# An mLSTM cell and a gated MLP in one kernel: who issues the loads of xT, and where five kinds of small steps stand in the order

## The chip, the cores and the metric

The kernel runs on one core of a Trainium2 chip. A core has five engines that run beside each other: TensorE (PE in the profile; its weight loads are PEld), VectorE (DVE), ScalarE (ACT), GpSimd (POOL) and SyncE (SP), which here only issues DMAs. Each engine works through its own instructions in the order in which they were written; an engine that must wait for another stands still until the semaphore arrives, and with it all that is queued behind. The metric is the device time of one launch in microseconds, lower is better; the times shown are medians of several runs.

## The reference

An mLSTM cell over 4 batches, 8 heads, 768 time steps and heads of 40 numbers, and behind it an MLP on the result, seen as 3072 tokens of 320 features:

```python
for t in range(S):
    m_new = np.maximum(f_gate[:, :, t] + m, i_gate[:, :, t])
    f_stab, i_stab = np.exp(f_gate[:, :, t] + m - m_new), np.exp(i_gate[:, :, t] - m_new)
    C = f_stab * C + i_stab * outer(v_t, k_t)      # 40 x 40 for each batch and head
    n = f_stab * n + i_stab * k_t
    h = C @ q_t
    y_t = sigmoid(o_gate_t) * h / np.maximum(np.abs(n @ q_t), 1.0)

x = y as (3072, 320)
h = x @ w_in                                       # 320 -> 2048
out = (h - np.tanh(h)) @ w_out                     # 2048 -> 320
```

## The kernel before, in words

**Units and groups.** The cell is cut into 24 units of 128 time steps of one batch (unit n is chunk n // 4 of batch n % 4). Within a unit the recurrence is a masked product of scores, P, with scaled values, vs, plus the product of the queries with the state that the batch's last unit left. Two units make a group of 256 tokens for the MLP; there are 12 groups. A group's input, transposed to features by tokens, is xT. The MLP works on the 2048 hidden features in 8 pairs of 128 + 128; an *item* is two pairs of one group: products up (ph_up <- xT, w_in), the polynomial for h - tanh(h) on ScalarE and VectorE (z, q, gt), products down (pS <- w_out or weight sums, gt or sums of gt), which run one item later.

**Seven products for eight.** From group 4 on, the 2 x 2 blocks of the up product and of the down product are computed with seven products in place of eight. That needs sums of weights (sum_w_in writes part or sums_in; sums_of_weights writes wT), sums of the inputs (sum_x, into freed xT buffers) and sums of gt (sums_of_g, s), all on VectorE.

**Two stretches.** The first 12 units and the first four groups are put in order by a small planner (class Plan) that simulates the engines. The second stretch, from item START = 17 on (about 203 us in the trace), is written out by a loop: for each item x it has a list of TensorE steps with costs (dense) and a list of other steps with places (work[x]), and merge() walks through both; a step placed at START + 0.8 comes when 0.8 of the first item's cost is through. Clock.later(key, us, step) holds a step back until that many microseconds of cost have been issued, or until Clock.need(key) asks for it.

**Slots.** In the second stretch the 12 units 12 to 23 pass through slots two items long (about 18.7 us). cell_slot(s, o) starts unit s (its loads, the scaling of its values in prepare) and finishes unit o, the one before: its four gate steps (gate_turned: den, o, ys, ys) and turn_by_store. A slot has 21 places (the last, which starts no unit, 20). For unit s the scores are computed in the slot's first item (crossed_scores: products ps, then two masks on VectorE that write P), and in the second item block_turned computes the state products (pT) and the products of P and vs.

**Through DRAM.** The unit's result stands in a layout with heads apart. turn_back transposes blocks of it on VectorE (zt), stores them with four DMAs (h_rows) and loads them again with four (z_in), all issued by SP. The gate steps of the next slot read z_in. turn_by_store then transposes y by blocks (yt), stores it with four DMAs (y_rows) and loads it as xT with three (96, 64 and 32 KB), these too issued by SP. SP's order in a slot is: loads of the next unit, y_rows of the unit before, xT of the unit before, h_rows of the slot's unit, z_in.

**GpSimd** has two memsets per slot in this stretch: zeros behind k, when the next unit's loads are issued, and zeros behind vs (the padding of the values), in block_turned.

**The order of an engine** is kept by a wrapper (Pinned, T) that chains every instruction to the one before on its engine; so nearly all instructions carry the wrapper's lines in the profile, L106 for VectorE, ScalarE, GpSimd and SP, L129 and L133 for TensorE. The names of tiles tell them apart.

**Banks.** An item's up products fill two PSUM tiles (X and Y in up_in_seven). Two adds (both), two squares (z) and two cubes (gt <- ph_up, z) read them; when the cubes and adds are through, the next item's first up product may write there:

```python
            square_b = square(z[0][:, 1], b, 0)
            add_d = V.tensor_tensor(out=both[:, 0], in0=d, in1=cs, op=OP.add)
            after(square(z[0][:, 0], a, 1), add_d)
            after(V.tensor_tensor(out=both[:, 1], in0=e, in1=cs, op=OP.add), square_b)
```

The masks of a new unit are issued right behind these lines, and steps given to Clock.later come behind the masks.

Of the kernel before, what the change touches and what calls it, by code (L numbers as in the profile page):

```python
# [60 lines left out]
L = 128  # L61
# [18 lines left out]
def kernel(  # L80
# [188 lines left out]
    B, NT, D, H, _ = qT.shape  # L269
    D1 = D + 1  # L270
# [6 lines left out]
    NK = 2  # L277
# [352 lines left out]
    def begin(n):  # L630
        if n in ld:
            arrive(n)

        un[n]["P"] = att.tile([L, 2, HH, L], FP, name="P", tag="P", bufs=4)
# [5 lines left out]
    def prepare(n, whole=True, by_heads=False):  # L640

        t = un[n]
        if "vs" in t:
            return
        t["vs"] = scaled(n, 0, "vs", 4, by_heads)
        if whole:
            t["column"]()
            open_gate(n)
# [147 lines left out]
    def turn_by_store(n):  # L796

        y, g, tt = un[n]["y"], *divmod(n, GT)  # L800
        yt = att.tile([L, NB, BLOCK], FP, name="yt", tag="yt", bufs=1)
        flat = yt.rearrange("p b j -> p (b j)")
        V.transpose(flat[:, 0:NK * 128], y[:, 0:NK * 128])
        V.transpose(flat[:, NK * 128:], y[:, FROM[NK]:DM])
        rows = dram.tile([DM, L], FP, name="y_rows", tag=f"y_rows{n % 4}")
        for a in range(L // BLOCK):
            part = slice(a * BLOCK, (a + 1) * BLOCK)
            SP.dma_start(out=rows[:, part].rearrange("(b i) j -> i b j", i=BLOCK), in_=yt[part])
        for i in range(2):
            half, to = slice(i * HALF, (i + 1) * HALF), xT[slot_of(g)][i * HALF:(i + 1) * HALF, :, tt * L:(tt + 1) * L]  # L810
            if i == 0:
                SP.dma_start(out=to, in_=bass.AP(rows.tensor, rows.offset, [[L, HALF], [128 * L, NK + 1], [1, L]]))
            else:
                SP.dma_start(out=to[:, 0:NK], in_=rows[0:NK * 128].rearrange("(c p) t -> p c t", p=128)[half])
                SP.dma_start(out=to[:, NK], in_=rows[FROM[NK]:])

    def in_halves(b):

# [10 lines left out]
    def block_turned(n):  # L829

        t = un[n]
        G.memset(t["wide"][:, H * D1:], 0.0)
        old = state[t["b"]][(t["c"] + 1) % 2].rearrange("p h d -> p (h d)")

        t["turned"] = [ps_a.tile([128, 2 * 2, L], FP, name="pT", tag=f"a{i}") for i in range(2)]
        for g in range(2):
            for c in range(2):
                for i in range(2):  # L840
                    rows, j = slice(i * HALF, i * HALF + D), 2 * g + c
                    T.matmul(t["turned"][i][c * HALF:(c + 1) * HALF, i * 2 + g, :], old[rows, j * D1:j * D1 + HALF], t["qz"][rows, j, :],
                             start=(g == 0), stop=False, skip_group_check=True)
        for i in range(2):
            P = over_diagonal(t["P"], i)
            for kind, half in ((0, 0), (1, 0), (0, 1), (1, 1)):
                for c in range(2):
                    g, r = i ^ kind, half ^ kind
                    rows, at = slice(r * HALF, (r + 1) * HALF), (i * HH + 2 * g + c) * D1
                    to = t["turned"][r][c * HALF:(c + 1) * HALF, i * 2 + g, half * HALF:]  # L850
                    T.matmul(to if half else to.rearrange("d (two t) -> d two t", two=2), t["wide"][rows, at:at + HALF],
                             P[rows, 1 + kind, c] if half else P[rows, 0:2 + kind:1 + kind, c], start=False, stop=True, skip_group_check=True)
        update_halves(n)
# [68 lines left out]
    def cell_slot(s, o):  # L922


        steps, pause = [], [(0.0, lambda: None)]
        if s is not None:
            if s + 1 < NU and s + 1 not in ld:
                load_unit(s + 1, ("kz", "qz", "v", "k", "o"), crossed=True)
            begin(s)
        if o is None:  # L930
            return [(0.0, lambda: prepare(s))]
        steps += 5 * pause
        if s is not None:
            steps.append((0.0, lambda: prepare(s)))
        steps += 6 * pause
        gates = []
        steps.append((0.0, lambda: [gates.extend(gate_turned(o)), gates[0]()]))
        steps += [(0.0, lambda i=i: gates[i]()) for i in range(1, 4)]
        steps.append((0.0, lambda: turn_by_store(o)))
        return steps + 4 * pause  # L940


    gT, po = {}, {}
# [18 lines left out]
    def sums_of_weights(p):  # L962
        if p % 2 == 0:
            both = conv.tile([128, 2, 4, HM], FP, name="wT", tag="w64", bufs=4)
            wT[p], wT[p + 1] = both[:, 0], both[:, 1]
        t = wT[p]
        even, odd = (w_out[:, 2 * p + i, :].rearrange("p (two n) -> p two n", two=2) for i in range(2))
        sub = OP.subtract
        return [(1.0, lambda o=o, a=a, b=b: V.tensor_tensor(out=o, in0=a, in1=b, op=sub)) for o, a, b in (
            (t[:, 0], even[:, 1], even[:, 0]), (t[:, 1], odd[:, 1], t[:, 0]),  # L970
            (t[:, 2], odd[:, 1], even[:, 1]), (t[:, 3], odd[:, 0], t[:, 1]))]
# [179 lines left out]
    def sum_w_in(p):  # L1151

        a11, a21, a12, a22 = (w_in[:, p, i * 128:(i + 1) * 128] for i in range(4))
        t = sums_in_of(p)
        both = w_in[:, p, 0:4 * 128].rearrange("p (j f) -> p j f", j=4)
        return [lambda: V.tensor_tensor(out=t[:, 0:4:2], in0=both[:, 1:4:2], in1=both[:, 0:2], op=OP.subtract),
                lambda: V.tensor_tensor(out=t[:, 1], in0=a22, in1=t[:, 0], op=OP.subtract),
                lambda: V.tensor_tensor(out=t[:, 3], in0=a12, in1=t[:, 1], op=OP.subtract)]
# [16 lines left out]
    def up_in_seven(x, some):  # L1175
# [43 lines left out]
        def shrunk():  # L1219
            both = conv.tile([128, 2, n, L], FP, name="both", tag="w_r", bufs=2)  # L1220
            z, q = ([mlp.tile([128, 2, n, L], FP, name=name, tag=name) for i in range(2)] for name in ("z", "q"))
            gt = gT[some] = [mlp.tile([128, 2, n, L], FP, name="gt", tag="gt", bufs=4) for i in range(2)]
            columns = [2 * x, 2 * x + 1, 2 * len(items) + x - START]

            def square(to, src, i):
                return A.activation(out=to, in_=src, func=AF.Square, accum_out=sums[:, columns[i]:columns[i] + 1])

            def again(i):
                A.activation(out=q[i], in_=z[i], func=AF.Square, bias=tiny)

            def cube(to, src, by):
                V.scalar_tensor_tensor(out=to, in0=src, scalar=TINY_POLY[0], in1=by, op0=OP.mult, op1=OP.mult)

            def last(i):
                V.scalar_tensor_tensor(out=gt[i], in0=q[i], scalar=TINY_POLY[2], in1=gt[i], op0=OP.add, op1=OP.mult)

            def after(later, sooner):
                tc.add_manual_dep(later.ins, sooner.ins.name, SYNC, reason="one engine at a bank")
# [5 lines that stand above are left out]
            again(0)  # L1244
            square(z[1], both, 2)
            again(1)
            early, late = (some, "early"), (some, "late")
            Clock.later(early, 1.0, lambda: cube(gt[0][:, 1], b, z[0][:, 1]))
            Clock.later(early, 1.1, lambda: cube(gt[0][:, 0], a, z[0][:, 0]))
            Clock.later(early, 1.9, lambda: last(0))  # L1250
            Clock.later(late, 2.6, lambda: cube(gt[1], both, z[1]))
            Clock.later(late, 3.3, lambda: last(1))
            Clock.later(some, 3.4, lambda: sums_of_g(some))
# [439 lines left out]
    def spread_over(steps, x0, x1):  # L1693

        for i, (cost, step) in enumerate(steps):
            at = x0 + i * (x1 - x0) / len(steps)
            work[int(at)].append((at, cost, step))
# [4 lines left out]
        x0, x1 = (START + (last - START) * j / len(slots) for j in (i, i + 1))  # L1702
        begins[int(x0)].append((slot, x0, x1))
    for p in range(2, SPLIT):
        spread_over([(0.0, lambda p=p: [step() for _, step in sums_of_weights(p)])], START + 0.8 + p / 2, START + 1.3 + p / 2)
    for p in range(NP - 2, NP):
        spread_over([(0.0, lambda step=step: step()) for step in sum_w_in(p)], START + p - 4.9, START + p - 4.4)
    for g in range(FIRST + 1, NG):
        spread_over([(0.0, lambda g=g: sum_x(g))], item(g * NP) - 0.7, item(g * NP) - 0.5)
    banks[:] = [name for name in ("b0", "b1") if name != third["tag"]]  # L1710
# [234 lines left out]
```

## Time and profile before

| | |
|---|---|
| runs | 512.88, 513.5, 520.36 us; median 513.5 |
| profiled execution | 512.03 us, span 510.2 us, mean granted TensorE clock 0.994 |
| busy, TensorE / VectorE / ScalarE / GpSimd | 97% / 82% / 51% / 8% of the span |
| DMA | 46.93 MB, mean 92 GB/s |
| chain that ended last, by engine | TensorE 80%, VectorE 8%, DMA 4%, SP 3%, ScalarE 2% |

The span is the time from the first to the last instruction of the profiled execution; its own time holds 1.8 us around it. Rows in order of time begin with the start in us and the duration in us, then the engine, the operation, the tile written and the tiles read, the shape, the number of instructions, and in brackets the idle time of the engine before the row with what ended it. Rows of waits are: engine, waiting tile, what it waited for, then the total in us, how often, and the longest. SPq is SP's queue of DMA issues: the duration there is that of the issue, not of the transfer. A group of DMA_DIRECT2D rows under POOL is GpSimd's time for its issues.

### The profile page before, as it was taken

The page shows a single profiled execution, that of the slowest core. Times are in us where ns is not written, and L with a number is a line of the kernel's source. Part 1 is how long each engine was busy: PE and PEld are TensorE (multiplying, and loading weights), DVE is VectorE, ACT ScalarE, POOL GpSimd, SP SyncE. Part 2 cuts the span into 40 slices and gives each one's busy share as a digit, 9 for nine tenths or more (in the row PEclk, how much of TensorE's full clock was granted, in tenths as well). Part 3 has the DMA queues.
Part 4 walks back from the last instruction along what each step waited for, and adds up shares of the span by engine and source line. Part 5 has one row for each costly group of instructions (what it writes and reads, how often), then busy time and mean ns, then how long its engine had stood idle before and what let it go on. Part 6 is the DMA issues. An engine that isn't in the chain of part 4 may idle for free.

```text
span 510.2 us, 12423 instructions
## 1 busy us (share of the span) xinstructions
PE 496.6 (97%) x4709; PEld 443.0 (87%) x4709; DVE 417.3 (82%) x1001; ACT 262.5 (51%) x709; POOL 41.2 (8%) x88
## 2 busy tenths in 40 slices
PE   9999999999999999999999999999999999899995
PEld 5778878887898989898999999999998999799985
DVE  5999979998887668699889898987987888676853
ACT  4575697676443424445455455464464464354640
POOL 4423323320000000000000000000000000000000
PEclk9999999999999999999999999999999999989998
DMA  7987645425001200024444445444434432320001
GB/s 232 279 266 234 190 133 174 155 70 80 8 2 38 62 27 26 2 55 94 97 98 101 88 104 107 96 100 94 90 88 95 97 89 36 57 55 1 28 1 31
DMA packets 109546, 46.93 MB, mean 92 GB/s; under 512 B 84201, under 2 KB 103209, under 8 KB 109481
## 3 DMA queue, kind: packets, MB, share of 16 engines
q1 hardware_dynamic: 103248, 31.33, 26.7%
q0 software_dynamic: 3040, 10.82, 6.7%
q10 hardware_dynamic: 3192, 3.93, 2.2%
q8 instruction: 39, 0.64, 0.5%
q14 instruction: 27, 0.21, 0.1%
HBM read 36.75 MB, written 9.04 MB: 90 GB/s over the span
## 4 chain that ended last, share of the span: by engine, by line
PE 80%; DVE 8%; DMA 4%; SPq 3%; ACT 2%; issue 2%; POOL 1%; DVEq 0%; ACTq 0%
PE ph_up L129 35%; PE pS L129 26%; PE po L129 7%; PE ph L129 4%; PE ps L129 3%; SPq L106 3%; PE pc L129 2%; PE pT L129 2%; DMA z_in<-h_rows 2%; PE awake L129 2%; DMA h_rows<-zt 1%; DVE gt L106 1%; DVE s L106 1%; DVE den L106 1%; PE px L133 1%
## 5 line engine op out<-in xcount | busy, mean ns | idle before, releaser
L129 PE MATMUL ph_up<-xT,w_in 64*64 64x256 f32 (+3 forms) x1276 | 171.2, 356 | 0.0
L129 PEld LDWEIGHTS ph_up<-xT,w_in 128*128 128x128 f32 (+2 forms) x1276 | 126.8, 168 | 20.0 <-issue 4.8
L106 ACT ACTIVATE z<-ph_up 128x256 f32<-128x256 f32 (+1 forms) x98 | 44.2, 451 | 127.3 <-PE ph_up L129 109.2
L129 PE MATMUL pS<-wT,s 128*128 128x160 f32 x480 | 81.2, 301 | 0.0
L106 ACT ACTIVATE q<-z,tiny 128x512 f32<-128x512 f32 (+1 forms) x98 | 69.8, 714 | 3.0
L106 DVE SCALAR_TENSOR_TENSOR gt<-q,gt 128x512 f32<-128x512 f32 (+1 forms) x98 | 65.6, 684 | 5.6 <-ACT q L106 0.6
L129 PEld LDWEIGHTS pS<-wT,s 128*128 128x128 f32 x480 | 69.4, 191 | 0.4 <-issue 0.3
L106 ACT COPY ph_up<-ph_up 128x256 f32<-128x256 f32 x93 | 33.3, 358 | 62.1 <-PE ph_up L129 42.7
L106 DVE SCALAR_TENSOR_TENSOR gt<-ph_up,z 128x256 f32<-128x256 f32 (+1 forms) x98 | 46.3, 498 | 18.1 <-ACT z L106 17.6
L129 PE MATMUL pS<-w_out,gt 128*128 128x160 f32 x320 | 55.3, 315 | 2.0 <-DVE ob L106 2.0
L129 PEld LDWEIGHTS pS<-w_out,gt 128*128 128x128 f32 x320 | 45.4, 192 | 8.6 <-issue 3.6
L106 DVE TENSOR_TENSOR both<-ph_up,cs 128x256 f32<-128x256 f32 x62 | 24.9, 419 | 26.3 <-PE ph_up L129 24.2
L129 PE MATMUL ph_up<-xT,sums_in 128*128 128x128 f32 x256 | 40.2, 280 | 2.4 <-DVE gt L106 2.4
L129 PEld LDWEIGHTS ph_up<-xT,sums_in 128*128 128x128 f32 x256 | 34.4, 191 | 4.7 <-issue 3.0
L129 PE MATMUL po<-w_out,gt 128*128 128x320 f32 x128 | 38.2, 441 | 0.0
L129 PE MATMUL ph_up<-xT,part 128*128 128x128 f32 x240 | 36.7, 275 | 1.1 <-DVE gt L106 1.1
L129 PEld LDWEIGHTS ph_up<-xT,part 128*128 128x128 f32 x240 | 32.4, 191 | 1.3 <-issue 1.3
L106 DVE TENSOR_TENSOR s<-gt 128x256 f32<-128x256 f32 x80 | 30.4, 420 | 1.1
L129 PEld LDWEIGHTS po<-w_out,gt 128*128 128x128 f32 x128 | 23.0, 190 | 8.5 <-issue 0.3
L129 PE MATMUL pS<-wT,gt 128*128 128x160 f32 x160 | 28.8, 303 | 0.0
L129 PE MATMUL pS<-w_out,s 128*128 128x160 f32 x160 | 28.3, 299 | 0.0
L129 PEld LDWEIGHTS ps<-qz,kz 40*64 40x64 f32 (+1 forms) x576 | 22.7, 151 | 2.7 <-DVE inv L106 0.4
(131 smaller groups left out, 704.1 us busy)
## 6 DMA issues: line engine op xcount, KB each, us to landing
w<-in_moe_w_out POOLq DMA_DIRECT2D x8, 640.0 KB, 6.6
w<-in_moe_w_in POOLq DMA_DIRECT2D x16, 256.0 KB, 4.7
kz<-in_kT SPq DMA_DIRECT2D x48, 80.0 KB
o<-in_o_gate SPq DMA_DIRECT2D x24, 160.0 KB
qz<-in_qT SPq DMA_DIRECT2D x44, 80.0 KB
out<-ob ACTq DMA_DIRECT2D x11, 320.0 KB
h_rows<-zt SPq DMA_DIRECT2D x48, 64.0 KB
z_in<-h_rows SPq DMA_DIRECT2D x48, 64.0 KB
```

The source lines that it names most:

```text
L106: i = method(*args, **kwargs)
L129: return cls.keep(nc.tensor.matmul(*args, **kwargs))
L133: return cls.keep(nc.tensor.transpose(*args, **kwargs))
```

## The change

Five edits, all in the second stretch. The three loads of xT in turn_by_store are issued by GpSimd in place of SP. The memset of the values' padding moves from block_turned to the place of prepare in the slot. The gate steps and turn_by_store stand one place later in the slot. The first two cubes of an item are issued right behind the adds, so ahead of the two masks of a new unit. The sums of the down weights for pairs 2 and 3 go from places START + 1.8 and START + 2.3 to START + 0.2 and START + 0.5, and the sums of w_in for pair 6 from START + 1.1 to START + 0.05 (those for pair 7 stay at START + 2.1).

```diff
@@ turn_by_store @@
             if i == 0:
-                SP.dma_start(out=to, in_=bass.AP(rows.tensor, rows.offset, [[L, HALF], [128 * L, NK + 1], [1, L]]))
+                G.dma_start(out=to, in_=bass.AP(rows.tensor, rows.offset, [[L, HALF], [128 * L, NK + 1], [1, L]]))
             else:
-                SP.dma_start(out=to[:, 0:NK], in_=rows[0:NK * 128].rearrange("(c p) t -> p c t", p=128)[half])
-                SP.dma_start(out=to[:, NK], in_=rows[FROM[NK]:])
+                G.dma_start(out=to[:, 0:NK], in_=rows[0:NK * 128].rearrange("(c p) t -> p c t", p=128)[half])
+                G.dma_start(out=to[:, NK], in_=rows[FROM[NK]:])
@@ block_turned @@
         t = un[n]
-        G.memset(t["wide"][:, H * D1:], 0.0)
         old = state[t["b"]][(t["c"] + 1) % 2].rearrange("p h d -> p (h d)")
@@ cell_slot @@
+        def ready():
+            prepare(s)
+            G.memset(un[s]["wide"][:, H * D1:], 0.0)
+
         if o is None:
-            return [(0.0, lambda: prepare(s))]
+            return [(0.0, ready)]
         steps += 5 * pause
         if s is not None:
-            steps.append((0.0, lambda: prepare(s)))
-        steps += 6 * pause
+            steps.append((0.0, ready))
+        steps += 7 * pause
         ...
         steps.append((0.0, lambda: turn_by_store(o)))
-        return steps + 4 * pause
+        return steps + 3 * pause
@@ up_in_seven @@
-            Clock.later(early, 1.0, lambda: cube(gt[0][:, 1], b, z[0][:, 1]))
-            Clock.later(early, 1.1, lambda: cube(gt[0][:, 0], a, z[0][:, 0]))
+            cube(gt[0][:, 1], b, z[0][:, 1])
+            cube(gt[0][:, 0], a, z[0][:, 0])
             Clock.later(early, 1.9, lambda: last(0))
@@ the loop @@
     for p in range(2, SPLIT):
-        spread_over([(0.0, lambda p=p: [step() for _, step in sums_of_weights(p)])], START + 0.8 + p / 2, START + 1.3 + p / 2)
+        spread_over([(0.0, lambda p=p: [step() for _, step in sums_of_weights(p)])], START + 0.3 * p - 0.4, START + 0.3 * p - 0.3)
     for p in range(NP - 2, NP):
-        spread_over([(0.0, lambda step=step: step()) for step in sum_w_in(p)], START + p - 4.9, START + p - 4.4)
+        spread_over([(0.0, lambda step=step: step()) for step in sum_w_in(p)], START + (0.05, 2.1)[p - NP + 2], START + (0.1, 2.6)[p - NP + 2])
```

## The prediction

> **What bounds the kernel now.** I read the page first, then the second stretch (from 203 us on, where the diff acts), in the order: TensorE's waits, its instructions in order of time, VectorE's beside them, SP's queue, GpSimd's.
>
> ```profile
> span 510.2 us, 12423 instructions
> PE 496.6 (97%) x4709; PEld 443.0 (87%) x4709; DVE 417.3 (82%) x1001; ACT 262.5 (51%) x709; POOL 41.2 (8%) x88
> ```
>
> TensorE is busy in 496.6 of 510.2 us. Its idle time is 13.6 us, and whatever this diff can win has to come out of that, or out of matmuls that run slower than they should. The waits of TensorE alone, from 200 us on, say how much of it lies in the stretch that the diff edits:
>
> ```profile
> PE ph_up L129 <- DVE gt L106: 3.5, 4, 1.1
> PE pS L129 <- DVE ob L106: 2.0, 1, 2.0
> ```
>
> Five waits (columns: total, times, longest), 5.5 us in all, every one of them for VectorE. TensorE's instructions in order of time put them in place (the bracket is the idle time before the row and what ended it):
>
> ```profile
> 211.88 0.68 PE L129 MATMUL ph_up<-xT,sums_in 128*128 128x128 f32 x4 [1.14 <-DVE gt L106]
> ...
> 231.80 0.68 PE L129 MATMUL ph_up<-xT,part 128*128 128x128 f32 x4 [1.07 <-DVE gt L106]
> ...
> 355.02 0.68 PE L129 MATMUL ph_up<-xT,sums_in 128*128 128x128 f32 x4 [0.41 <-DVE gt L106]
> ...
> 392.60 0.68 PE L129 MATMUL ph_up<-xT,sums_in 128*128 128x128 f32 x4 [0.84 <-DVE gt L106]
> ...
> 445.48 2.33 PE L129 MATMUL pS<-w_out,gt 128*128 128x160 f32 x8 [2.02 <-DVE ob L106]
> ```
>
> The fifth has a tail. Eight of those matmuls take 2.33 us there, and stretches of one microsecond give the granted clock (the column before the last two):
>
> ```profile
> 445.00:446.00 1.00, 0.52 (x3) 0.52 (x3) 0.93 (x4) 0.00 (x0) 0.00 (x0) 0.85 0.00 0
> 446.00:447.00 1.00, 1.00 (x5) 1.00 (x5) 1.00 (x4) 0.00 (x0) 0.00 (x0) 0.50 0.00 0
> ...
> 448.00:449.00 1.00, 1.00 (x6) 1.00 (x5) 0.70 (x3) 0.97 (x3) 0.00 (x0) 0.50 0.53 82
> 449.00:450.00 1.00, 1.00 (x10) 1.00 (x10) 1.00 (x2) 0.97 (x3) 0.00 (x0) 0.95 0.59 96
> ```
>
> After 2.02 us without work the clock was 0.50 for three whole stretches, 0.85 and 0.95 in those around them: 0.15 + 3 x 0.50 + 0.05 = 1.70 us lost on top. After the stalls of 1.14 us and less nothing of the kind is seen. So the five stalls are worth 1.14 + 1.07 + 0.41 + 0.84 + 2.02 + 1.70 = 7.18 us of this execution. Everything else in the stretch is TensorE working without a gap, and nothing in the diff takes a matmul away. 7.2 us is therefore about the most that the edits can give.
>
> The page "TensorE: Matmul & The Clock Gate" of the Trainium skill (Part 1, What's actually happening) gives the idle window before the clock halves as about 3.4 us; by that, a stop of 2.02 us would cost no clock, the ceiling would be 5.48 us and the sum below 5.3 in place of 7.0. The rows with 0.50 say otherwise here, and I count the 1.70.
>
> **The change part by part.** *Cubes ahead of masks.* VectorE's rows before the first stall:
>
> ```profile
> 209.18 0.97 DVE L106 TENSOR_TENSOR both<-ph_up,cs 128x256 f32<-128x256 f32 x2 [3.94 <-PE ph_up L129]
> 210.06 1.01 DVE L106 TENSOR_TENSOR P<-ps,over 128x384 f32<-128x384 f32 x2
> 210.99 0.74 DVE L106 SCALAR_TENSOR_TENSOR gt<-ph_up,z 128x256 f32<-128x256 f32 x2
> ```
> ```profile
> 217.65 0.62 PE L129 MATMUL pT<-qz,state 40*64 40x128 f32 x16
> ```
>
> The two adds (both) wait 3.94 us for TensorE, then come the two score masks (P), then the two cubes (gt<-ph_up), and it is the cubes that free the banks in which the next item's first product is written. The masks' result is read only by the next item's state products (pT), at 217.65, more than 6 us after the masks' end. With the cubes first they start at 210.06 in place of 210.99: 0.93 us earlier, and TensorE with them. Do the cubes have their squares by then? The first square is done before the second add may start; the second square follows the first add (209.18 + 0.49) and takes one activation, which I put at no more than an add: 210.2, while the first cube runs. The stall of 1.14 shrinks by **0.93**. Nothing is added: the same instructions, two of them 0.74 us later, in twelve items.
>
> *Weight sums moved.* The second stall, at 231.80, follows a VectorE that has had no gap since 209; among its rows is
>
> ```profile
> 227.65 0.32 DVE L106 TENSOR_TENSOR wT<-w_out 128x160 f32<-128x160 f32 x1
> ```
>
> the start of four sums of 0.32 us (1.06 us from start to start of what follows). Those for pairs 2 and 3, and the three sums of w_in for pair 6 (0.42 + 0.28 + 0.28), go up to 2 items ahead, to the item that begins at 203: about 3.3 us of work, placed before the adds of 209.18, where VectorE waits 3.94 us. It fits with some 0.6 us to spare; if it did not, the first stall would grow by the excess. With 1.06 us gone directly before the stall, more gone earlier, and 0.93 from the masks, all **1.07** of it goes. Price of the placing if the cover is gone: those 3.3 us beside a TensorE that waits, under 1 us here.
>
> *xT loads on GpSimd.* SP's queue is served in order. Its waits have this row (total, times, longest):
>
> ```profile
> SPq L106 <- DMA y_rows<-yt: 26.1, 14, 2.9
> ```
>
> The three loads of xT wait until the four stores of y_rows have landed, and everything behind them on SP waits too: the four stores of the next unit's h_rows, though zt is ready, then the loads of z_in, then the gate on VectorE. Two units, VectorE's side and SP's:
>
> ```profile
> 375.40 0.65 DVE L106 STREAM_TRANSPOSE zt<-zt 128x448 f32<-128x448 f32 x1
> ...
> 388.00 0.17 DVE L106 SCALAR_TENSOR_TENSOR den<-z_in,inv 128x8 f32<-128x8 f32 x1 [1.98 <-DMA z_in<-h_rows]
> ...
> 431.03 0.65 DVE L106 STREAM_TRANSPOSE zt<-zt 128x448 f32<-128x448 f32 x1
> ...
> 441.86 0.17 DVE L106 SCALAR_TENSOR_TENSOR den<-z_in,inv 128x8 f32<-128x8 f32 x1 [2.82 <-DMA z_in<-h_rows]
> ...
> 444.94 0.48 DVE L106 TENSOR_TENSOR ob<-pS,a 128x320 f32<-128x320 f32 x1
> ```
> ```profile
> 378.81 3.76 SPq L106 DMA_DIRECT2D h_rows<-zt  x4
> ...
> 428.19 1.81 SPq L106 DMA_DIRECT2D y_rows<-yt  x4
> 432.65 1.89 SPq L106 DMA_DIRECT2D xT<-y_rows  x3
> 434.64 2.15 SPq L106 DMA_DIRECT2D h_rows<-zt  x4
> 438.28 1.90 SPq L106 DMA_DIRECT2D z_in<-h_rows  x4
> ```
>
> zt of the last unit is written at 431.68 (431.03 + 0.65); SP is through with y_rows at 430.00; but h_rows go out at 434.64, behind the xT loads. Without these they go at 431.7, 2.9 us sooner, and the z_in on which VectorE stood for 2.82 us is there at 438.9 in place of 441.8, before VectorE is free to ask for it (it began to wait at 439.04). For the unit of 388.00 the store can go at 376.05 in place of 378.81: 2.76 us sooner against a wait of 1.98. So the waits behind the stalls at 355, 392 and 445 end, and with them **0.41 + 0.84 + 2.02 + 1.70 = 4.97 us**. What is late next at 445: the partial result (ob), which VectorE does after three sums of g (1.6 us) and the gate (den, o, ys: about 1.5 us): 439.04 + 3.1 + 0.48 = 442.6, while TensorE can use the bank at 443.46. It holds by 0.8 us.
>
> What the move adds is on GpSimd. Its issues as far as the trace shows them are weight loads (min/median/max in ns, then landing in us):
>
> ```profile
> L106 POOL DMA_DIRECT2D w<-in_moe_w_in x32: 526/538/776, 4.6 to 86.8; - x32
> L106 POOL DMA_DIRECT2D w<-in_moe_w_out x8: 717/732/1255, 7.3 to 105.0; - x8
> DMA to landing us min/median/max: 3.1/5.1/8.7
> ```
>
> Three loads (96, 64 and 32 KB) at 0.54 to 0.73 us are 1.6 to 2.2 us per unit on an engine that does this here and no more:
>
> ```profile
> 352.46 0.12 POOL L106 MEMSET vs<- 128x23 f32 x1 [18.57 <-DVE xT L106]
> ```
>
> SP took 1.9 us for the same three, so the issue costs the same; the landing is unknown, and I bound it by 3.1 and 8.7 us and take the lower end, since those weight loads of 64 to 640 KB ran against a much busier DMA. Who waits for xT? The sums of x for the next group and its first product. The last unit is the tightest:
>
> ```profile
> 452.09 1.88 SPq L106 DMA_DIRECT2D xT<-y_rows  x3
> ```
> ```profile
> 460.94 0.48 DVE L106 TENSOR_TENSOR xT<-xT 128x128 f32<-128x128 f32 x2
> ```
>
> From the landing of y_rows (452.09) to the sum 8.9 us pass; the stall at 445 delayed the first more than the second, so I reckon with some 7. Issue 1.6 to 2.2 plus landing 3.1 is 5: hidden. With 8.7 it is 10.9, and the group begins up to 4 us late. The five other groups have 10 us and more.
>
> Behind the waiting loads on GpSimd stand the memsets of k's and the values' padding of the next unit. They are read 1.5 items, over 10 us, later, and both of a slot are now issued before its loads: cost nothing. Without that move the memset would stand behind a load that waits, and the products of the state behind it; that is why I give it no time of its own.
>
> *Gate one place later.* A place is a 21st of a slot of 18.7 us, 0.9 us. It only moves den, o and ys behind 0.9 us of other work; the turned y, its store and its load are 0.9 us later, out of the 7 above. Alone it would take 0.9 us off each wait of 2 us; with z_in early it gives nothing. Zero.
>
> A row and a rule on the GpSimd side. In the first stretch, four issues and VectorE beside them, and one issue beside another form:
>
> ```profile
> 45.27 2.16 POOL L106 DMA_DIRECT2D w<-in_moe_w_in  x4 [1.38 <-DVE w_e L106]
> ...
> 87.38 1.25 POOL L106 DMA_DIRECT2D w<-in_moe_w_out  x1
> ```
> ```profile
> 44.90 0.68 DVE L106 SCALAR_TENSOR_TENSOR gt<-ph_up,z 128x512 f32<-128x512 f32 x1
> ...
> 87.60 0.48 DVE L106 TENSOR_SCALAR w_e<-w 128x640 int32<-128x640 int32 x1
> ```
>
> Products with two sources ran at their usual 0.68 us through four issues of 0.54. Next to TENSOR_SCALAR the issue took 1.25 in place of 0.73. The page "SBUF — State Buffer" of the Trainium skill (Who interferes with whom, and its summary's advice to issue a DMA from ACT or SP when VectorE is at work) says that the issue on GpSimd is locked out while VectorE copies or does tensor_scalar, and not by tensor_tensor. Read as advice for all of VectorE's work it would take 3 x 0.52 = 1.6 us of the last unit's 7 and make the late xT below a case of 0.2; the rows agree with its narrow wording, VectorE has neither form in the second stretch before the closing count, and I leave that case at 0.12.
>
> **The sum.** 0.93 + 1.07 + 4.97 = 6.97 us. Against the profiled execution, 512.03 us (span 510.2 and 1.8 around it), that is 505.1. The timed runs were 512.88, 513.5 and 520.36; the two close ones lie 0.9 and 1.5 above the profiled one, so a median of about **506.3**.
>
> **The rivals.**
>
> *xT comes late at the last group.* Landing at 8.7: 3 to 4 us of wait and up to 1.7 of clock, about 5: 506.3 + 5 = 511. It decides from a landing of 5 us on. For it speaks that no load of xT by GpSimd is in the trace; against it, how small these three are beside the weight loads.
>
> *The loads were not what held h_rows.* That the move then doesn't do what it is said to: if h_rows wait for something else, the gate still waits, and only the first two stalls go: 506.3 + 5 = 511. Against it: at 434.64 the store starts within 0.1 us of the last xT issue (432.65 + 1.89), and in the 388 unit likewise.
>
> *Slower: VectorE stands still while GpSimd issues.* Place: three issues in each of 12 slots. Price: if they block as long as the longest issue (1.25 us), 3.8 us per slot. VectorE is 82% busy (the page's row), so a slot of 18.7 us has 3.4 us free, of which I let half absorb a block: 2 us per slot reach TensorE, 12 x 2 = 24 us, 506 + 24 = 530. It turns to a loss against today once more than 0.6 us per slot (7 us over 12) get through, and to over 2% from 1.5 us on. Against it: the 0.68 us above.
>
> *More than that.* A median as near to the profiled run as the closest run today (0.9 in place of 1.2 us) and short waits inside the items that no record names, for which I allow 2 us, as VectorE gets ahead: 503 to 504.
>
> **How the numbers follow.** Forecast 0.68 (its own range 504.5 to 508); late xT 0.12 and blocked stores 0.08, both at 509 to 512; slower 0.05; more 0.07. The range 503 to 512 leaves out the slower case, and parts of the others. A measurement here tells 2%, 10.3 us, from no change. Faster by that needs 503.2 or less: 0.07. Slower by it needs 523.8: 0.04. Within: 0.89.
>
> **What would show it.** Right: from 200 us on TensorE's waits for VectorE fall from 5.5 us to under 1; SP no longer waits for y_rows and GpSimd does; den waits for z_in in few places or none; the clock stays at 1.00 around 440; the masks stand behind the cubes; 3.3 us of sums fill the gap before 209. Wrong: a wait of sums of x or first products for xT near 452 to 460; an issue on GpSimd above 1 us with VectorE's products longer beside it; a new wait of TensorE at the items where masks went back.

## Result and profile after

| | before | after |
|---|---|---|
| median of the runs | 513.5 us | 505.46 us |
| range | 512.43 to 521.9 us, 5 runs | 504.71 to 516.49 us, 5 runs |
| after / before | | 0.9845, 95% interval 0.9822 to 0.9867 |

The change saves 1.55%, about 8 us; 506.3 us and a change within 2% had been forecast. In some executions, among them the profiled ones of the changed kernel, e4, e12 and e13, TensorE's first 28 to 31 us run at about half pace and the second stretch begins 10 to 11 us later, so the ratios leave the long runs out (six of e6's twelve). Traces are compared from a mark behind that stretch: from the first product of the second stretch that reads a sum of weights (sums_in) to the last pS<-w_out,s. TensorE's instructions in order of time, before and then after:

```profile
203.11 0.61 PE L129 MATMUL ph_up<-xT,sums_in 128*128 128x128 f32 x4
...
504.11 0.71 PE L129 MATMUL pS<-w_out,s 128*128 128x160 f32 x4
```
```profile
214.27 0.61 PE L129 MATMUL ph_up<-xT,sums_in 128*128 128x128 f32 x4
...
508.10 0.71 PE L129 MATMUL pS<-w_out,s 128*128 128x160 f32 x4
```

Between the marks lie 301.00 us before and 293.83 us after: 7.17 us less, where the sum of the prediction had 6.97 and its ceiling 7.18. After's largest wait, TensorE's and SP's waits in the same stretch (total, times, longest):

```profile
POOL xT L106 <- DMA y_rows<-yt: 181.7, 11, 17.7
...
PE ph_up L129 <- DVE gt L106: 0.7, 2, 0.5
```
```profile
SPq L106 <- DVE yt L106: 63.5, 11, 10.3
```

TensorE waits for VectorE 0.7 us in two places, where it waited 5.5 us in five. The wait for y_rows has left SP and stands on GpSimd, where it is 181.7 us long and no engine's wait for GpSimd is listed. SP now waits for work to be written (yt), and h_rows follow y_rows at once:

```profile
362.45 2.70 SPq L106 DMA_DIRECT2D y_rows<-yt  x4
365.25 2.04 SPq L106 DMA_DIRECT2D h_rows<-zt  x4
368.77 1.90 SPq L106 DMA_DIRECT2D z_in<-h_rows  x4
```
```profile
370.25 0.74 DVE L106 SCALAR_TENSOR_TENSOR gt<-ph_up,z 128x256 f32<-128x256 f32 x2
370.92 1.01 DVE L106 TENSOR_TENSOR P<-ps,over 128x384 f32<-128x384 f32 x2
...
375.56 0.16 DVE L106 SCALAR_TENSOR_TENSOR den<-z_in,inv 128x8 f32<-128x8 f32 x1
```

These rows of SP and VectorE show one slot. z_in is issued at 368.77 to 370.67; den comes to it at 375.56 and waits for nothing (no bracket). The cubes (gt) stand ahead of the masks (P). And ten microseconds around the last stall, before around 445 and after around its place there, 453 (the granted clock stands in the third column from the end):

```profile
440.00:450.00 10.00, 7.98 (x58) 7.09 (x57) 7.58 (x22) 3.78 (x11) 0.00 (x0) 0.83 0.23 37
```
```profile
450.00:460.00 10.00, 9.50 (x85) 8.28 (x78) 7.03 (x18) 4.78 (x15) 1.73 (x3) 1.00 0.27 71
```

TensorE is busy for 9.50 of 10 us in place of 7.98: a stall of 0.50 us is left there, and the clock stays at 1.00.

GpSimd's issues of xT and their landing (mean ns of one; then KB each and median us to landing):

```profile
L106 POOL DMA_DIRECT2D xT<-y_rows x36 | 20.7, 581 | 273.2 <-DMA y_rows<-yt 181.7 <-PE ph_up L129 91.5
```
```profile
xT<-y_rows POOLq DMA_DIRECT2D x12, 96.0 KB, 2.4
xT<-y_rows POOLq DMA_DIRECT2D x12, 32.0 KB, 1.9
```

An issue costs 0.58 us, and the data are there in 1.9 to 2.4 us, below the lower of my two bounds (3.1).

### The profile page after: what moved, and what is told of

It is laid out like the page before. It is cut to its first block, busy times and chain, and to the rows that moved or that the text cites. A ratio compares the mean times of both kernels' runs of the same rounds, so it can differ in the third digit from the quotient of the medians.

```text
span 514.6 us, 12450 instructions
## 1 busy us (share of the span) xinstructions
PE 505.9 (98%) x4709; PEld 449.8 (87%) x4709; DVE 416.0 (81%) x1001; ACT 262.2 (51%) x709; POOL 62.0 (12%) x124
## 4 chain that ended last, share of the span: by engine, by line
PE 93%; DVE 4%; ACT 1%; issue 1%; DVEq 0%; ACTq 0%
PE ph_up L129 39%; PE pS L129 30%; PE po L129 7%; PE ph L129 5%; PE ps L129 4%; PE awake L129 3%; PE pT L129 3%; PE pc L129 2%; PE px L133 1%; DVE gt L106 1%; DVE w_in L106 0%; ACT vs L106 0%; DVE ob L106 0%; PE gate L129 0%; DVE w_e L106 0%
## 5 line engine op out<-in xcount | busy, mean ns | idle before, releaser
L106 POOL DMA_DIRECT2D xT<-y_rows x36 | 20.7, 581 | 273.2 <-DMA y_rows<-yt 181.7
L129 PEld LDWEIGHTS ph<-vs,P 128*128 128x128 f32 x192 | 27.7, 217 | 1.2 <-issue 0.8
```

The lines of the kernel that those rows point to most:

```text
L106: i = method(*args, **kwargs)
L129: return cls.keep(nc.tensor.matmul(*args, **kwargs))
```

## The experiments

The theories at first were the prediction's: each edit takes its own stall away, and SP's queue delays z_in by a fixed time. The runs put another in their place, called the loop below.

**e1, the xT loads alone.** Before, with the loads and the memset of the padding as changed:

```diff
-                SP.dma_start(out=to, in_=...)      # and the two others
+                G.dma_start(out=to, in_=...)
```

> Kernel before with one edit: the loads of xT on GpSimd (with the padding's memset in its new place, which the loads need). Theory (the xT loads block SP's queue): h_rows go out when zt is ready, den waits for z_in nowhere, the stalls at 355, 392 and 445 and the slow clock behind the last are gone, those at 211 (1.14 us) and 231 (1.07 us) stay: 4.97 us faster, ratio 0.990. Rival 1 (something else holds h_rows): den still waits 10.8 us, no change, ratio 1.000. Rival 2 (GpSimd's issues stop VectorE): products with two sources next to an issue take 0.5 us or more longer than 0.68 us, ratio above 1.

506.75 us median, ratio 0.9843 [0.9786, 0.9900]. TensorE's waits for VectorE and the two marks:

```profile
PE ph_up L129 <- DVE gt L106: 2.2, 2, 1.1
```
```profile
205.52 0.61 PE L129 MATMUL ph_up<-xT,sums_in 128*128 128x128 f32 x4
...
501.10 0.71 PE L129 MATMUL pS<-w_out,s 128*128 128x160 f32 x4
```

Only the first two stalls stay (2.2 us); den waits nowhere. Between the marks 295.58 us: 5.42 less than before, where 4.97 was expected. This edit carries most of the gain.

**e2, the cubes ahead of the masks alone.**

```diff
-            Clock.later(early, 1.0, lambda: cube(gt[0][:, 1], b, z[0][:, 1]))
+            cube(gt[0][:, 1], b, z[0][:, 1])      # and the other cube
```

> Kernel before with one edit: the cubes right behind the adds. Theory (the order of VectorE frees the banks late): the stall at 211 goes from 1.14 to about 0.2 us, that at 231 from 1.07 to about 0.15; where y is turned ahead of the cubes the banks come 0.5 us sooner too, so 355 goes from 0.41 to 0 and 392 from 0.84 to about 0.35; 445 stays at 2.0 with its slow clock: 2.7 us faster, ratio 0.995. Rival (the cubes have to wait for their squares): VectorE stands still ahead of the cubes for up to 0.9 us in each of the twelve items with masks, and the stalls stay, ratio 1.000 or above.

518.36 us, ratio 1.0071 [1.0033, 1.0108]: slower, against the theory, and not by the rival's way, since the cubes wait for their squares no more than before. The stall at 211 did shrink, from 1.14 to 0.21 us, but den's waits doubled from 10.8 us, and the marks lie 306.59 us apart. In VectorE's rows the cubes (gt) now stand between den and the turning of y (yt):

```profile
DVE den L106 <- DMA z_in<-h_rows: 21.6, 11, 3.6
```
```profile
355.58 0.75 DVE L106 SCALAR_TENSOR_TENSOR gt<-ph_up,z 128x256 f32<-128x256 f32 x2
356.24 0.56 DVE L106 STREAM_TRANSPOSE yt<-ys 128x256 f32<-128x256 f32 x2
```

**e3, the weight sums alone.**

```diff
-  ... sums_of_weights(p) ..., START + 0.8 + p / 2, START + 1.3 + p / 2)
+  ... sums_of_weights(p) ..., START + 0.3 * p - 0.4, START + 0.3 * p - 0.3)      # and sum_w_in
```

> Kernel before with one edit: the weight sums in their new places. Theory: they fit into VectorE's 3.94 us of waiting before the adds of 209; the stall at 211 stays 1.14, that at 231 goes from 1.07 to 0, the others stay: 1.1 us faster, ratio 0.998. Rival (they don't fit): the adds at 209 come late and the stall at 211 grows by up to 1 us, which takes the gain back, ratio 1.000.

513.54 us, ratio 0.9963 [0.9926, 0.9999]. The stalls at 231 and 392 are gone and the one at 211 stays at 1.14 us, so the sums fit. But the marks are 300.93 us apart, only 0.07 us less than before, where 1.1 us had been expected: den's waits grew to 13.5 us, a stall of 0.65 us came at 335, the large one at 445 went from 2.02 to 2.29 us, and TensorE's busy time between the marks grew from 295.52 to 296.37 us. What was won early was lost later.

**e4, the gate one place later alone.**

```diff
-        steps += 6 * pause
+        steps += 7 * pause
```

> Kernel before with one edit: the gate one place later. Theory: each wait of den for z_in shrinks by up to 0.9 us and those below that vanish; the stall at 355 goes, 392 goes from 0.84 to 0, 445 shrinks from 2.0 to about 1 us and keeps or loses its slow clock: 2 to 4 us faster, ratio 0.992 to 0.996; so it does part of what the loads do, and nothing beside them. Rival (it is in order behind other work that is late as well): no stall moves, ratio 1.000.

521.43 us, ratio 1.011 [1.004, 1.018]: slower too, where the theory had 0.992 to 0.996 and the rival 1.000. The marks lie 306.20 us apart.

```profile
DVE den L106 <- DMA z_in<-h_rows: 20.3, 11, 3.0
```

den asks 0.9 us later and waits longer, 20.3 us in place of 10.8. A wait with a fixed end can't do that. So z_in itself came later, and the reason has to run through the gate. **The loop:** here is one turn of it in the kernel before, VectorE's side and SP's.

```profile
292.22 0.17 DVE L106 SCALAR_TENSOR_TENSOR den<-z_in,inv 128x8 f32<-128x8 f32 x1 [0.40 <-DMA z_in<-h_rows]
...
350.43 0.17 DVE L106 SCALAR_TENSOR_TENSOR den<-z_in,inv 128x8 f32<-128x8 f32 x1 [2.15 <-DMA z_in<-h_rows]
...
353.68 0.56 DVE L106 STREAM_TRANSPOSE yt<-ys 128x256 f32<-128x256 f32 x2
...
367.99 0.17 DVE L106 SCALAR_TENSOR_TENSOR den<-z_in,inv 128x8 f32<-128x8 f32 x1 [0.27 <-DMA z_in<-h_rows]
...
424.35 0.17 DVE L106 SCALAR_TENSOR_TENSOR den<-z_in,inv 128x8 f32<-128x8 f32 x1 [0.77 <-DMA z_in<-h_rows]
```
```profile
354.26 1.85 SPq L106 DMA_DIRECT2D y_rows<-yt  x4
358.77 1.92 SPq L106 DMA_DIRECT2D xT<-y_rows  x3
360.79 2.16 SPq L106 DMA_DIRECT2D h_rows<-zt  x4
364.42 1.91 SPq L106 DMA_DIRECT2D z_in<-h_rows  x4
```

den of unit o (350.43) leads to yt (353.68), to the stores of y_rows (354.26), to the xT loads, which wait until these have landed (358.77), to h_rows of the next unit s behind them on SP (360.79), to z_in (364.42), and to den of unit s (367.99). That den begins the next turn: the gate of one slot is fed by the gate of the slot before. If the turn takes longer than TensorE's own 18.54 us for a slot (the period of the changed kernel, where den waits nowhere), the turn sets the pace. From the fourth den to the eleventh, seven slots, before takes 424.35 - 292.22 = 132.13 us, 18.88 a slot. Each edit alone changes what VectorE does between den and yt, and that is part of the turn.

**e11, the gate one place earlier.** This was to show that a gate moved the other way shortens the turn.

```diff
-        steps += 6 * pause
+        steps += 5 * pause
```

> The kernel before with one edit against the direction of the change: the gate steps and turn_by_store stand one place EARLIER. Theory of the loop (gate of unit o -> y_rows -> xT loads on SP -> h_rows of unit s behind them -> z_in -> gate of unit s, one slot later): one turn of the loop is about 0.6 us shorter (the gate one place later made the period from den to den 19.49 in place of 18.88 us), so about 18.3 us, less than TensorE's own 18.54 us per slot. The waits of den for z_in shrink from 10.8 us in 10 to under 5 us, TensorE's stalls at 355, 392 and 445 go, those at 211 and 231 stay; 2 to 5 us less than before, ratio 0.990 to 0.996. Rival (the wait is one-way, as my prediction read it: z_in comes when it comes, and a gate that asks 0.9 us sooner waits 0.9 us longer): den's waits grow to 18 us or more and the time is the same or longer, ratio 1.000 to 1.005.

522.73 us, ratio 1.0151 [1.0104, 1.0198]. The turn did not get shorter, and this expectation fell. The rival's direction held, and by more than its 1.000 to 1.005, but not its reason, since z_in didn't come when it had come before: the period grew to 19.82 us. VectorE's rows between den and yt say why:

```profile
353.02 0.17 DVE L106 SCALAR_TENSOR_TENSOR den<-z_in,inv 128x8 f32<-128x8 f32 x1 [2.03 <-DMA z_in<-h_rows]
...
353.55 0.64 DVE L106 SCALAR_TENSOR_TENSOR gt<-q,gt 128x512 f32<-128x512 f32 x1
354.22 0.76 DVE L106 TENSOR_TENSOR s<-gt 128x256 f32<-128x256 f32 x2
...
357.98 0.57 DVE L106 STREAM_TRANSPOSE yt<-ys 128x256 f32<-128x256 f32 x2
```

A product of the item (gt<-q) and the sums of gt (s) now stand between the gate's own steps, and from den to yt 4.96 us pass, where before had 3.25. The place as such isn't what counts, but what VectorE has to do between den and yt.

**e12, the gate's five steps in one place.** Loads still on SP, gate at its old place, nothing between den and yt:

```diff
-        steps += [(0.0, lambda i=i: gates[i]()) for i in range(1, 4)]
-        steps.append((0.0, lambda: turn_by_store(o)))
-        return steps + 4 * pause
+        # all four gates and turn_by_store in the step of gates[0]
+        return steps + 8 * pause
```

> The kernel before, the xT loads still on SP ahead of h_rows and the gate at its old place, but its four steps and turn_by_store stand in one place in place of five, so that VectorE does nothing else between den and yt (before: sums of x, adds of the next item; from den to yt 3.25 to 4.0 us). Theory of the loop, with its turn set by what VectorE does between den and yt (one place later 4.7 to 5.4 us, one place earlier 5.0 to 5.5 us, both slower): den to yt falls to about 1.9 us, the turn from 18.9 to about 17.2 us, under TensorE's own 18.54 us; den's waits for z_in fall from 10.8 us to under 2, the period from den to den comes to 18.54 to 18.6 us, TensorE's stalls at 355, 392 and 445 go; ratio 0.988 to 0.994. Rival (no loop: SP's order delays z_in by a fixed time, and the two gate experiments were slower because the gate's neighbours were): den's waits stay at 10 us or more, ratio 0.998 to 1.008.

508.94 us, ratio 0.991 [0.988, 0.994], by an edit that touches neither SP's order nor GpSimd.

```profile
358.06 0.16 DVE L106 SCALAR_TENSOR_TENSOR den<-z_in,inv 128x8 f32<-128x8 f32 x1
...
359.81 0.57 DVE L106 STREAM_TRANSPOSE yt<-ys 128x256 f32<-128x256 f32 x2
```
```profile
PE ph_up L129 <- DVE gt L106: 2.2, 2, 1.1
```

From den to yt 1.75 us; den waits for z_in nowhere, TensorE keeps the first two stalls alone, as in e1, and 296.32 us lie between the marks. From the rows of den and yt of the fourth to the tenth turn (means), and the dens from the fourth to the eleventh:

| kernel | den to yt, us | den to den, us |
|---|---|---|
| before | 3.68 | 18.88 |
| e2, cubes | 4.33 | 19.43 |
| e3, sums | 3.68 | 18.93 |
| e4, gate later | 5.11 | 19.49 |
| e11, gate earlier | 5.26 | 19.82 |
| e12, gate at once | 1.76 | 18.61 |
| e13, gate at once, cubes, sums | 1.77 | 18.70 |
| e1, loads on GpSimd | 3.71 | 18.55 |
| after | 5.21 | 18.54 |

With the loads ahead of h_rows the period grows with the first column; with the loads on GpSimd it is TensorE's 18.54 us even with 5.21 us from den to yt. The rest of the turn was 15.20 and 15.10 us in before and e2, but 14.38 and 14.56 us in e4 and e11. Most of the difference lies between the first store of y_rows and the first load of xT, so in the landing of that store: 4.35 us in before, 3.65 in e4 and 3.81 in e11 (means of the same turns). In e2 it was 4.02, but there h_rows to z_in took 4.65 us in place of 4.12. Why the landings differ is open.

**e5, the changed kernel with the gate at its old place.**

```diff
-        steps += 7 * pause
+        steps += 6 * pause
```

> The changed kernel with the gate steps at their old place. Theory of the loop: with the xT loads off SP the loop is open, so the place of the gate costs and gives nothing: ratio to before as for the changed kernel, 0.984 to 0.987, no wait of den for z_in above 0.3 us in sum, period from den to den 18.54 us. Rival (the later gate is needed to cover z_in also now): den waits for z_in by up to 0.9 us in several slots, stalls of TensorE beside them, 1 to 4 us more, ratio 0.987 to 0.993.

504.98 us, ratio 0.9813 [0.9768, 0.9859]. Its marks:

```profile
203.29 0.61 PE L129 MATMUL ph_up<-xT,sums_in 128*128 128x128 f32 x4
...
496.73 0.71 PE L129 MATMUL pS<-w_out,s 128*128 128x160 f32 x4
```

293.44 us, 0.39 less than after. With the loop open the gate's place gives nothing and costs nothing that can be measured; the ratio lies a little below the 0.984 to 0.987 expected, which its interval covers.

**e6, the loads on SP, but behind h_rows.**

```diff
+        behind_stores.append(lambda: load_back(rows, g, tt))      # turn_by_store
...
+        while behind_stores:                                      # turn_back, behind h_rows
+            behind_stores.pop()()
```

> The changed kernel with the three xT loads on SP again, but issued behind the next four h_rows in place of ahead of them. Theory (it is the order in SP's queue that cost, not the engine that issues): h_rows go out as soon as zt is written, y_rows have landed long before, so SP does not stand; den has no wait for z_in, or some tenths since z_in now stands behind three issues of 0.6 us; ratio 0.984 to 0.988. Rival (GpSimd's issue is needed, because SP has too little free time and z_in comes 1.9 us later behind the xT issues): den waits 0.5 to 1.5 us per slot, stalls of TensorE return, ratio 0.990 to 0.998.

509.89 us as the median of all twelve runs, ratio 0.9826 [0.9786, 0.9865]; 293.64 us between the marks; no wait of den. Which engine issues makes no difference here; the place in SP's queue was the cause. The page "DMA: Bandwidth & Descriptors" of the Trainium skill (Issuing engines are not separate DMA queues) says that issuing from several engines saves only the time of the issue. Here a move to another engine was worth 5.42 us; e6 agrees that the engine itself is not what gave them.

**e9, the changed kernel with the gate one more place later.**

```diff
-        steps += 7 * pause
+        steps += 8 * pause
```

> The changed kernel with the gate steps one more place later. Theory: with the loop open nothing waits for the gate but the last group's xT, which has some 5 us of slack; the last stall of 0.50 us (at 453, VectorE's turned y ahead of the adds) may go or move: ratio within 0.001 of the changed kernel. Rival (the place is tuned: later steps push the partial result or the last xT): new stalls of 0.5 to 2 us, ratio up by 0.001 to 0.005.

505.65 us, ratio 0.9819 [0.9765, 0.9874], not to be told from e5. The stall of 0.50 us is gone and 496.29 - 203.32 = 292.97 us lie between the marks.

**e13, gate at once with cubes and sums, the loads still on SP ahead of h_rows.** The diffs of e2, e3 and e12 together.

> The kernel before with the gate's five steps in one place, the cubes ahead of the masks and the weight sums moved; the xT loads stay on SP ahead of h_rows and the padding stays in block_turned. Theory of the loop: den to yt is 1.76 us as with the gate in one place alone, so the turn is about 17 us and TensorE's 18.54 us decide; the cubes, which cost 5.6 us alone, now give what the prediction priced them at, 0.9 us, and the sums 1.1 us; from the first to the last of the two marked products 294 to 295 us (the gate in one place alone 296.3), ratio 0.983 to 0.988. Rival (the cubes ahead of the masks push the masks and what follows, whatever the loop does, and need the loads on GpSimd): den waits for z_in again or new stalls of TensorE come, 297 to 302 us, ratio 0.991 to 1.000.

506.34 us, ratio 0.985 [0.9816, 0.9884]; between the marks 509.17 - 214.27 = 294.90 us. den waits 2.4 us in three slots, TensorE 0.7 us in all. The cubes and sums together, which alone cost 5.59 and gave 0.07 us, here give 296.32 - 294.90 = 1.42 us, with the loads still on SP. The loop is shorter, but not open: one turn took 358.82 - 338.35 = 20.47 us, in which SP was still issuing the next unit's loads when yt was written (1.70 us), and the first xT load came 3.19 us after the last y_rows had been issued.

**e7, the loads on GpSimd, the memset left in block_turned.**

```diff
-                SP.dma_start(out=to, in_=...)      # as e1, without the move of the memset
+                G.dma_start(out=to, in_=...)
```

> The kernel before with the xT loads on GpSimd, the memset of the values' padding left in block_turned. Theory: the memset then stands on GpSimd behind the loads, which wait for y_rows; the products of P and vs wait until about 8 us after their time in each of 11 slots, and TensorE with them, with up to 1.7 us of slow clock after each stop: 80 to 110 us more than the loads with the memset moved (506.8), so 590 to 617 us. Rival (the memset's place does not matter, the write needs no more than its own 0.14 us somewhere): 506 to 512 us.

One run: 613.11 us. TensorE's largest waits, GpSimd in order of time, and TensorE beside it:

```profile
PE pT L129 <- POOL vs L106: 41.5, 6, 7.7
...
PE pT L129 <- POOL k L106: 35.1, 5, 8.7
```
```profile
388.69 1.72 POOL L106 DMA_DIRECT2D xT<-y_rows  x3 [27.34 <-DMA y_rows<-yt]
390.40 0.14 POOL L106 MEMSET vs<- 128x23 f32 x1
```
```profile
390.60 0.91 PE L129 MATMUL pT<-P,vs 64*64 64x128 f32 x14 [7.62 <-POOL vs L106]
```

A memset of 0.14 us, queued behind loads that wait, costs 41.5 + 35.1 = 76.6 us of stops in eleven slots (vs and k name the two memsets that stand together behind the loads). Against e1 the run is 613.11 - 506.75 = 106 us longer; most of the rest is the clock, which after the ends of the eleven stops stays at half speed for 54.4 us in all, so 27 us lost.

**e8, two more DMAs by GpSimd for each unit.** The extra ones copy the same rows to a scratch tile.

```diff
+            G.dma_start(out=bass.AP(spare_rows...), in_=bass.AP(rows...))      # 96 KB
+            G.dma_start(out=spare_rows[...][half], in_=rows[...][half])        # 64 KB
```

> The changed kernel with two more DMAs of the same rows (96 and 64 KB, to a scratch tile that nobody reads) issued by GpSimd behind the three xT loads of each unit: five issues in place of three. Theory (an issue on GpSimd holds nobody up): VectorE's products with two sources stay at 0.68 us, ratio to before as for the changed kernel within 0.002. Rival (VectorE stands still while GpSimd issues, hidden today by VectorE's free time): 1.2 us more per slot with VectorE's rows beside the issues longer, 3 to 14 us in all, ratio 0.991 to 1.010.

507.64 us in 4 runs, ratio 0.9898 [0.9866, 0.993]: between the two expectations. The expected 0.68 us is that of the products that write gt (685 ns in e8, 686 in after), but these hardly ever stand beside an issue. What does stand there shows in one slot, GpSimd's rows and VectorE's:

```profile
356.06 1.73 POOL L106 DMA_DIRECT2D xT<-y_rows  x3 [15.80 <-DMA y_rows<-yt]
357.78 1.20 POOL L106 DMA_DIRECT2D spare_rows<-y_rows  x2
```
```profile
355.75 0.42 DVE L106 TENSOR_TENSOR s<-gt,s 128x256 f32<-128x256 f32 x1
356.09 0.48 DVE L106 TENSOR_TENSOR vs<-v,crossed 128x320 f32<-128x320 f32 x1
358.38 0.96 DVE L106 TENSOR_TENSOR both<-ph_up,cs 128x256 f32<-128x256 f32 x2 [1.80 <-PE ph_up L129]
```

The sum and the scaling beside the issues take 0.42 and 0.48 us, as in before, the adds (both) 0.96 us, as half of them do in before, and for much of the issues VectorE waits for TensorE (1.80 us). The marks are 293.83 us apart, exactly as after. So 14.4 us of more issues cost VectorE nothing that the trace shows; a long product beside an issue was not tried. The profiled run has 504.9 - 497.10 = 7.80 us behind the last mark, where none of these issues run, and after 514.6 - 508.10 = 6.50; why two of the four runs took 2 us more is open, since those were not profiled.

No kernel tried beats the changed one by more than a measurement tells: e5, e6, e9 and e13 lie at 0.981 to 0.985.

## Why the prediction was right, and where it was not

*The ceiling and the sum.* The sum was right: 7.17 us between the marks against 6.97. By edits, from the marks: the loads 301.00 - 295.58 = 5.42 (predicted 4.97), cubes and sums on top of them 295.58 - 293.44 = 2.14 (predicted 0.93 + 1.07 = 2.00), the gate 293.44 - 293.83 = -0.39 (predicted 0). That it fits to 0.2 us is partly luck, since the gate takes back most of what the others gave beyond their price. The ceiling of 7.2 us was too low: after still has stalls of 0.7 us, and e5 and e9, which differ from it only in the gate's place, are 7.56 and 8.03 us below before. The stretch between the marks, before and after (TensorE's busy time stands behind the length):

```profile
203.11:504.11 301.00, 295.52 (x3400) 276.34 (x3399) 246.07 (x618) 148.97 (x421) 1.60 (x15) 0.99 0.32 71
```
```profile
214.27:508.10 293.83, 293.12 (x3400) 274.48 (x3399) 244.59 (x618) 149.00 (x421) 22.27 (x51) 1.00 0.32 73
```

TensorE's idle time fell by 4.77 us and its busy time by 2.40, of which the clock explains 1.70. By subtraction the other 0.70 us is in products that ran longer without a wait in the profile. "Everything else in the stretch is TensorE working without a gap" had counted them as nothing; the case *More than that* had allowed 2 us for them.

*The loads and SP's queue.* Right in place and in the way by which the loads hold h_rows; e1 and e6 show it. The rival that something else held h_rows is out: in after they start 0.1 us behind y_rows.

*"Alone it would take 0.9 us off each wait of 2 us."* Wrong: e4 made the waits longer and the kernel 1.1% slower. The step that failed is the reading of den's wait as one-way, with an end that the gate doesn't touch. The rows for the loop stood in the trace: the store behind yt, the loads that wait for it, h_rows behind these. I followed them forward from one den to the next wait, but not round to where the first den's own time came from.

*The cubes' 0.93 and the sums' 1.07 us.* Right only where the loop doesn't set the pace; the prediction didn't say that they depend on it. Beside the loads they give 2.14 us together, beside the gate in one place 1.42. Alone the cubes cost 5.59 us between the marks (306.59 - 301.00), as they push yt back behind them, and the sums win 0.07. The size of the sums was a little high, 3.3 us where the prediction's own rows give 2 x 1.06 + 0.98 = 3.10, but they fit either way: the stall at 211 didn't grow in e3.

*What the loads meet on GpSimd.* Late xT did not come: landing 1.9 to 2.4 us in place of the 3.1 I took. *VectorE stands still while GpSimd issues* did not come either: what runs beside the issues keeps its 0.42 and 0.48 us. But that is little work, since VectorE often waits for TensorE then, so how a long product would fare stays open. The padding's memset was given no time for the right reason: without its move the price is e7's.

## What to carry to other kernels

When a wait comes back in every round, ask whether the thing waited for depends, some queues further on, on the same engine's output of the round before; then sum the whole turn and compare it with the bound engine's own time per round. While the turn is the longer, work put between its start and its first store costs time, and edits that only fill gaps elsewhere can show nothing. Open the loop first, by the order in a queue or by keeping foreign work out of it, and judge the small edits afterwards.

## What was not expected of the hardware

A stop of 2.02 us cost clock and one of 1.69 us none, but the length of the stop isn't all that counts. Windows around stops of 2.29 us (e3), of 2.75 (e2), and of 1.69 and 3.20 (e11), with the mean granted clock in the third column from the end:

```profile
444.00:450.00 6.00, 4.37 (x22) 4.37 (x23) 5.59 (x16) 2.26 (x6) 0.00 (x0) 0.72 0.17 26
```
```profile
450.00:457.00 7.00, 5.43 (x29) 5.43 (x30) 6.47 (x17) 2.91 (x8) 0.00 (x0) 0.76 0.24 55
```
```profile
279.00:286.00 7.00, 5.02 (x39) 4.57 (x38) 6.21 (x18) 4.12 (x11) 0.00 (x0) 1.00 0.28 60
457.00:464.00 7.00, 6.45 (x36) 6.28 (x37) 6.42 (x16) 3.18 (x8) 0.00 (x0) 0.76 0.39 100
```

6 x 0.28 = 1.68 us are lost, and twice 7 x 0.24 = 1.68, like before's 1.70: as much behind a stop of 3.20 us as behind one of 2.02. Behind the stop of 1.69 us nothing is lost. At half speed 1.7 us of loss are a spell of some 3.4 us. Behind e7's eleven stops of 6.1 to 8.7 us the spells last 6.83 or 10.24 us, two or three times 3.41.

The falls keep a fixed step too. In stretches of 0.25 us of e7's trace the first six fall at 243.53, 270.83, 301.55, 328.86, 359.57 and 386.88 us, so 27.3 or 30.7 us apart: 8 or 9 times 3.41. Cut by that step from its fall at 458.74 us, e11's trace has a boundary at 281.25, inside the stop of 1.69 us, which leaves at most 1.41 us of standing still in one step. That fits a clock that is set once per step by how idle the step was, but it is not shown: e3's fall at 445.27 us came after a step with 1.93 us of standing still, a step with as much at the end of that run had none behind it, and e1's fall at 22.08 us came after a step with 1.03 us.

The page "TensorE: Matmul & The Clock Gate" of the Trainium skill (Part 1, What's actually happening) gives about 3.4 us of work for the way back to full speed, and the spells of 3.4 us agree; after e7's stops work ran at half clock for 3.2 to 6.5 us. It gives the same figure for the idle time that lowers the clock, and there the rows differ: 2.02 us were enough. How much of a step has to be idle, no run here tells.
